# Attention and two expert layers on one core: later planning of the q, k, v loads, half as many filling products, new due times

## The chip, the cores and the metric

The kernel runs on one core of a Trainium2 chip, in one launch. The metric is the device time of that core in microseconds (us): the median of 3 runs before the change is 1045.23 us (1044.54 to 1047.05).

## What is computed

```python
scores = where(block_i >= block_j, q @ k.T / sqrt(64), -1e9)   # 4 batches, 8 heads, 576 positions, blocks of 64
attn   = exp(scores - max) / (sum + 1e-9)
x      = (attn @ v) as 2304 tokens x 512
h      = x @ moe_w_in                    # 512 -> 2048
x      = (h * tanh(softplus(h))) @ moe_w_out        # 2048 -> 512
h      = max(x @ moe2_w_in, 0)
out    = (h * h) @ moe2_w_out
```

## The kernel before, in words

The 2304 tokens are six chunks of 384. The first two chunks hold the low positions (0 to 191) of all four batches and are made by `attention_lo`, the other four the high positions, by `attention_hi`. Each chunk then goes through layer 1 and layer 2, in the twelve passes of `PASSES`; a pass is 16 steps, each of 12 products in `first_half` (line 1028, x by w_in) and 12 in `second_half` (line 1061, g by w_out), 128 x 384 each. Together these are 4608 products, called the main products below. Numbers are split in a high and a low half of 16 bits, so that each product is done three times.

**Weights.** The weights come as 64-bit floats. `unit` (lines 892 to 937) makes one of 32 units ready: a load of 1 MB into `raw` (line 895, two buffers), three passes of VectorE over 1024 columns (lines 905, 906, 908), a square on ScalarE (line 911), four norm products into the bank `spare` (line 915), their maximum on VectorE (line 922), a few tiny steps, and the two halves (lines 868 and 571).

**A head pair of the first two chunks** (`attention_lo`): loads of q and k (line 781, tile `qk`, two buffers) and of v (line 783, tile `vs`), the score products (line 791, tile `acc`), maxima on VectorE (lines 805 to 808), three exponentials on ScalarE into the single buffer `pl` (line 811), the scaling on GpSimd (line 577), the high half `pb` on ScalarE (line 553), the low half by a subtraction on GpSimd or VectorE (lines 559, 560), a transposing DMA (line 825), the products with v (line 760), and their copy to `xs` (line 770) with a maximum (line 772). There are 16 such pairs. Behind the eight pairs of a chunk stands `chunk_scale` (line 973).

**The order.** All instructions are tasks of a planner, class `Sched`. It has a duration for each task and a due place (`rank`) from tables at the end of the file (`W_AT`, `A_AT`, `ATT` and others). `forward` runs a list schedule over the engines with these durations, `backward` ranks the tasks by the latest start, and the program is written in the order of the planned starts. So each engine, and SyncE's queue of DMA issues, executes its tasks strictly in the planned order, whatever the real times are. For two kinds of operation the planner also chooses the engine.

**Filling products.** Where TensorE is planned to be idle, `fill` counts how many 128 x 128 products with the constant `ones` would go into the gap, and the writer emits that number ahead of the next task (line 1233). Their results go to the second half of the bank `spare` and are read by nobody.

```python
        t.fillers = n, where
...
    for t in seq:
        for _ in range(t.fillers[0] if t.fillers else 0):
            nc.tensor.matmul(out=spare[t.fillers[1]][:, 1, 0:128], lhsT=ones, rhs=ones, start=True, stop=True)
        t.fn()
```

Of the kernel before, what the change touches and what calls it, by code (L numbers as in the profile page):

```python
# [18 lines left out]
B, H, S, D = 4, 8, 576, 64  # L19
# [53 lines left out]

W_AT = [[[4000.0, 4500.0], [45000.0, 4500.0]]]

# [26 lines left out]


class Task:
    __slots__ = ("eng", "dur", "fn", "deps", "succ", "lat", "pos", "prio", "n", "ready", "start", "lock", "idx", "post", "after", "before", "opts", "fin", "why", "gen", "xpose", "first", "rank", "rows", "final", "fillers", "table", "mark")


class Sched:
# [7 lines left out]
    FIRST = {"PE": 300.0, "ACT": 1300.0, "DVE": 700.0}  # L116
    FILL, GUARD = 0.0, 300.0
    ROUNDS = 2


    SWITCH, HYST = 1300.0, 6000.0
# [19 lines left out]

    def add(self, eng, dur, fn, r=(), w=(), lat=0.0, lock=False, deps=(), pos=None, opts=(), table=None):
        t = Task()
        t.opts, t.table, t.mark = opts, table, None
        t.eng, t.dur, t.fn, t.lat, t.lock = eng, dur, fn, lat, lock
        t.deps, t.succ, t.pos, t.idx = set(deps), [], pos, len(self.tasks)
        t.after, t.before, t.rows, t.final, t.fillers = set(), [], 1.0, None, None
        for acc, write in ((r, False), (w, True)):
            for a in acc:
                inst, reg = a if isinstance(a, tuple) else (a, None)  # L150
                regs = list(set(inst.wr) | set(inst.rd)) if reg is None else [reg, None]
                for g in regs:
                    t.deps.update(inst.wr.get(g, ()))
                    if write:
                        t.deps.update(inst.rd.get(g, ()))
        for acc, write in ((r, False), (w, True)):
            for a in acc:
                inst, reg = a if isinstance(a, tuple) else (a, None)
                if not inst.tasks or inst.tasks[-1] is not t:
                    inst.tasks.append(t)  # L160
                if write:
                    if reg is None:
                        inst.wr, inst.rd = {None: [t]}, {}
                    else:
                        inst.wr[reg], inst.rd[reg] = [t], []
                else:
                    inst.rd.setdefault(reg, []).append(t)
        t.deps.discard(t)
        self.tasks.append(t)
        return t  # L170
# [13 lines left out]
    def fill(self, now, start, t, where):  # L184

        n = 0
        while True:
            f = Task()
            f.dur, f.rows = self.FILL, 1.0
            busy = dict(self.busy)  # L190
            self.clock(f, now)
            if now + f.dur > start - self.GUARD:
                self.busy = busy
                break
            now += f.dur
            n += 1
        t.fillers = n, where

    def build(self, order):
        for ring in self.rings:  # L200
# [79 lines left out]
    def forward(self):  # L280
# [32 lines left out]
        dma = xpose = 0.0  # L313
# [6 lines left out]
        while len(done) < len(self.tasks):  # L320
            best = None
            for name, (free, wait, ready) in engs.items():
                for q in (wait, ready):
                    while q and q[0][-1].start is not None:
                        heapq.heappop(q)
                if not wait and not ready:
                    continue
                now = max(free, blocked.get(name, 0.0)) if ready else max(free, wait[0][0])
                if best is None or now < best[0]:
                    best = (now, name)  # L330
            now, name = best
            e = engs[name]
            while e[1] and e[1][0][0] <= now:
                t = heapq.heappop(e[1])[2]
                if t.start is None:
                    heapq.heappush(e[2], (*key(t), t))
            t, skipped = None, []
            while e[2]:
                item = heapq.heappop(e[2])
                if item[-1].start is not None:  # L340
                    continue
                if item[-1].opts and better(item[-1], name, now):
                    skipped.append(item)
                    continue
                t = item[-1]
                break
            if name == "ACT" and t is not None and t.table and table and t.table != table:
                other = [i for i in e[2] if i[-1].start is None and i[-1].table in (None, table) and not i[-1].opts
                         and i[-1].rank < t.rank + self.HYST]
                if other:  # L350
                    heapq.heappush(e[2], (*key(t), t))
                    t = min(other)[-1]
            for item in skipped:
                heapq.heappush(e[2], item)
            if t is None:
                blocked[name] = now + 100.0
                e[0] = max(e[0], now)
                continue
            start = now

            if name == "DVE" and self.CONTEND:
                over = engs["POOL"][0] - now
                if over > 0:
                    t.dur += min(over, t.dur) * self.CONTEND[0] if t.lock else self.CONTEND[1] if t.dur < 130.0 else 0.0
            elif name == "POOL" and self.CONTEND:
                t.dur += max(0.0, min(engs["DVE"][0] - now, t.dur)) * self.CONTEND[2]
            if name == "ACT" and t.table and t.table != table:
                if table:
                    start += self.SWITCH
                    self.switches += 1  # L370
                table = t.table
            if not self.lock_model:
                pass
            elif name == "POOL":
                start = max(start, port[0])
            elif name == "DVE" and t.lock:
                start = max(start, port[1])
            if name == "PE":
                if t.final:
                    self.spare[t.final] = False  # L380
                place_ = [k for k, free in self.spare.items() if free]
                if place_ and self.FILL:
                    self.fill(e[0], start, t, place_[0])
            t.start = start
            if name == "PE":
                self.clock(t, start)
            end = start + t.dur
            if name == "POOL":
                port[1] = end
            elif name == "DVE" and t.lock:  # L390
                port[0] = end
            e[0] = end
            fin = end + t.lat
            if name == "SP":
                if t.xpose:
                    end = max(end, xpose + 170.0)
                dma = max(dma, end + 650.0 - (t.dur - t.gen)) + t.post
                if t.xpose:
                    xpose = dma
                e[0] = max(end, dma - self.AHEAD)  # L400
                fin = dma
            done.append(t)
            for k, s in enumerate(t.succ + t.before):
                s.n -= 1
                rt = fin + self.SEM[t.eng][s.eng] if k < len(t.succ) else start + 1.0
                if rt >= s.ready:
                    s.ready, s.why = rt, t
                if not s.n:
                    place(s)
# [28 lines left out]
def tile_attention_moe(ctx, tc, qk, qp, va, vd, w1, w2, out):  # L438
    nc = tc.nc
# [101 lines left out]
    def dma(fn, nbytes, r=(), w=(), issue=475.0, gen=475.0):  # L541
        t = sch.add("SP", issue, fn, r=r, w=w, lat=650.0 - (issue - gen) + nbytes / DMAR)
        t.post, t.gen, t.xpose = nbytes / DMAR, gen, issue > 1000
        return t
# [17 lines left out]
    def flat(t):  # L562
        return t.rearrange("p c k -> p (c k)")
# [211 lines left out]
    def attention_lo(b, h, x, xo, s_bank, av_bank):  # L775
# [2 lines left out]
        qs, vs, v3 = (R[k].new() for k in ("qk", "vs", "v3"))  # L778
        scale = 0.125
        cost = lambda m: c_mm(4 * m)  # L780
        dma(lambda: nc.sync.dma_start(qs.t[0:64, 0:4 * n].rearrange("p (a s) -> p a s", s=n), qk[b, h // 2].rearrange("d h a s -> d (h a) s")),
            1024 * n, w=[qs], issue=650.0, gen=650.0)
        dma(lambda: nc.sync.dma_start(flat(vs.t)[:, 0:6 * D], vd[b, :, h // 2].rearrange("p c k -> p (c k)")), 128 * 1536, w=[vs])
        thirds(vs, v3)

        pp, st = s_bank(0).new(), R["st"].new()
# [344 lines left out]
    n = NX  # L1131
# [115 lines left out]


L2_AT = [78800.0, 5000.0]
W_AT = [[[4300.0, 4300.0], [44000.0, 6800.0]]]  # L1250
C0_AT = 46000.0
C1_AT = 77500.0
A_AT = [[0.0, 16500.0], [44500.0, 73700.0], [75100.0, 150000.0]]
ATT = [[2, 2, 0, 0.0, 1.08], [3, 2, 1, 1.34, 2.57], [4, 5, 7, 0.47, 2.61], [5, 5, 8, 2.07, 4.28]]
Sched.SLACK = 0.98
Sched.HYST = 9200.0

# [56 lines left out]
```

## Time and profile before

| | |
|---|---|
| median of 3 runs | 1045.23 us (1044.54 to 1047.05) |
| the profiled execution | 1044.21 us, its span 1042.4 us |
| busy PE, DVE, ACT, POOL | 980.4, 648.0, 631.8, 175.6 us |
| mean granted TensorE clock | 0.98 |
| DMA | 153.83 MB, mean 148 GB/s |

All times of the trace are microseconds from the start of the span. A busy TensorE (PE) is not a useful one: the filling products count as busy, and a matmul's end is modelled, so that neighbouring products overlap in the rows. The granted clock is the share of full speed (1.0 is 2.4 GHz, 0.5 is 1.2 GHz) that the throttle gave TensorE; over a stretch it is a mean of these two levels. A releaser in brackets is what ended an engine's idle time.

### The profile page before, as it was taken

The page shows a single profiled execution, that of the slowest core. Times are in us where ns is not written, and L with a number is a line of the kernel's source. Part 1 is how long each engine was busy: PE and PEld are TensorE (multiplying, and loading weights), DVE is VectorE, ACT ScalarE, POOL GpSimd, SP SyncE. Part 2 cuts the span into 40 slices and gives each one's busy share as a digit, 9 for nine tenths or more (in the row PEclk, how much of TensorE's full clock was granted, in tenths as well). Part 3 has the DMA queues.
Part 4 walks back from the last instruction along what each step waited for, and adds up shares of the span by engine and source line. Part 5 has one row for each costly group of instructions (what it writes and reads, how often), then busy time and mean ns, then how long its engine had stood idle before and what let it go on. Part 6 is the DMA issues. An engine that isn't in the chain of part 4 may idle for free. (4 is left out here: it accounts for less than half of the span.)

```text
span 1042.4 us, 19262 instructions
## 1 busy us (share of the span) xinstructions
PE 980.4 (94%) x7409; PEld 612.7 (59%) x7409; DVE 648.0 (62%) x1539; ACT 631.8 (61%) x1157; POOL 175.6 (17%) x222
## 2 busy tenths in 40 slices
PE   8778888998999999999989999999899999999997
PEld 7677656666654555555545555655455566666664
DVE  5657987898989766786566378465675552141211
ACT  4435688665767666678765677565677753354443
POOL 2223732311212111211111011001121110000000
PEclk8889999999999999999999999999999999999999
DMA  7636796886646585585552256564755431122322
GB/s 231 149 82 188 203 280 195 268 297 222 256 135 157 133 189 132 138 196 151 133 127 67 82 143 144 119 160 140 173 130 130 86 97 62 61 81 82 112 80 92
DMA packets 150716, 153.83 MB, mean 148 GB/s; under 512 B 120160, under 2 KB 125280, under 8 KB 146528
## 3 DMA queue, kind: packets, MB, share of 16 engines
q1 hardware_dynamic: 150624, 152.60, 53.1%
q8 instruction: 58, 0.95, 0.4%
q14 instruction: 34, 0.28, 0.1%
HBM read 109.58 MB, written 14.16 MB: 119 GB/s over the span
## 5 line engine op out<-in xcount | busy, mean ns | idle before, releaser
L1061 PE MATMUL acc<-g,ws 128*128 128x384 f16 x2304 | 462.6, 326 | 3.8 <-DMA ws<-wspill 2.5
L1061 PEld LDWEIGHTS <-ws 128*128 128x128 f16 x2304 | 223.1, 98 | 152.8 <-issue 4.6
L571 DVE SCALAR_TENSOR_TENSOR g<-h,cst,g 128x384 f16<-128x384 f32 x192 | 120.7, 630 | 204.9 <-ACT g L868 159.5
L1028 PE MATMUL hp<-x,res 128*128 128x384 f16 x1152 | 234.2, 329 | 2.5 <-ACT h L1034 2.3
L1034 ACT ACTIVATE h<-hp,cst 128x384 f32<-128x384 f32 x192 | 110.0, 576 | 165.7 <-PE hp L1028 165.0
L1028 PE MATMUL hp<-x,late 128*128 128x384 f16 x864 | 181.6, 326 | 0.8 <-DVE cst L996 0.8
L1028 PEld LDWEIGHTS <-res 128*128 128x128 f16 x1152 | 110.7, 99 | 79.7 <-issue 12.4
L869 POOL TENSOR_SCALAR g<-h,cst 128x384 f16<-128x384 f32 x85 | 62.0, 731 | 378.7 <-PE acc L1061 160.8
L1028 PEld LDWEIGHTS <-late 128*128 128x128 f16 x864 | 81.5, 98 | 59.5 <-issue 7.9
L1233 PE MATMUL spare<-ones 128*128 128x128 bf16 x1205 | 88.5, 240 | 26.6 <-DVE wst L922 18.1
L1233 PEld LDWEIGHTS <-ones 128*128 128x128 bf16 x1205 | 82.9, 109 | 33.2 <-issue 22.2
L670 ACT ACTIVATE pf<-pab,st,sq 128x320 f32<-128x320 f32 (+2 forms) x96 | 67.3, 702 | 34.2 <-DVE st L665 29.6
L571 DVE SCALAR_TENSOR_TENSOR pb<-pf,st,pb 128x384 f16<-128x384 f32 (+2 forms) x96 | 72.4, 764 | 20.8 <-ACT pb L688 20.2
L868 ACT ACTIVATE g<-h,cst 128x384 f16<-128x384 f32 x107 | 65.6, 613 | 29.1 <-PE acc L1061 23.9
L688 ACT ACTIVATE pb<-pf,st 128x384 f16<-128x384 f32 (+2 forms) x96 | 64.9, 714 | 21.1 <-DVE st L681 7.6
L1028 PE MATMUL hp<-x,ws 128*128 128x384 f16 x288 | 59.6, 332 | 2.2 <-ACT h L1034 2.2
L662 DVE TENSOR_REDUCE st<-pab 128x2 f32<-128x640 f32 (+2 forms) x48 | 49.9, 1039 | 3.2 <-PE pab L654 2.3
L902 ACT ACTIVATE wf<-raw 128x1024 f32<-128x1024 f32 x32 | 36.5, 1141 | 21.6 <-DMA raw<-in_w_dram 10.6
L577 POOL TENSOR_SCALAR pl<-pl,st 128x192 f32<-128x192 f32 (+1 forms) x48 | 35.4, 751 | 75.0 <-DVE st L816 24.4
L981 POOL TENSOR_SCALAR x<-xs,cst 128x384 f16<-128x384 f32 x29 | 24.6, 862 | 122.6 <-DVE cst L863 112.2
L1039 ACT ACTIVATE h<-h 128x384 f32<-128x384 f32 x85 | 43.8, 515 | 1.1
L654 PE MATMUL pab<-q 64*128 64x320 f16 (+3 forms) x384 | 39.6, 307 | 3.7 <-DVE q L571 1.5
(120 smaller groups left out, 1072.0 us busy)
## 6 DMA issues: line engine op xcount, KB each, us to landing
ws<-wspill SPq DMA_DIRECT2D x108, 512.0 KB, 3.8
raw<-in_w_dram SPq DMA_DIRECT2D x32, 1024.0 KB, 6.0
wspill<-wn SPq DMA_DIRECT2D x18, 512.0 KB, 4.7
qk<-in_qp_dram SPq DMA_DIRECT2D x16, 480.0 KB, 4.1
vs<-in_va_dram SPq DMA_DIRECT2D x16, 320.0 KB, 3.9
out_dram<-ev SPq DMA_DIRECT2D x24, 192.0 KB, 2.1
qk<-in_qk_dram SPq DMA_DIRECT2D x16, 192.0 KB, 4.2
vs<-in_vd_dram SPq DMA_DIRECT2D x16, 192.0 KB, 3.7
```

Of the source, the lines that this page charges most:

```text
L571: return sch.add("DVE", c_dve(n) + 62 * ap, lambda: nc.vector.scalar_tensor_tensor(dst(), a(), s() if ap else s, c(), op0, op1), r=r, w=w, ...
L654: nc.tensor.matmul(out=pp.t[:, hd, o:o + k1 - k0], lhsT=qh.t[rows, u, a:a + 128], rhs=qh.t[rows, w, nq + k0:nq + k1], start=p == 0, stop=p ...
L662: sch.add("DVE", c_dve(2 * (o1 - o0)), lambda: nc.vector.reduce_max(both(st, j, r0), pp.t[r0:, :, o0:o1], axis=AX.X), w=[(pp, 0), (st, j)])
L670: sch.add("ACT", c_act(o1 - o0, True, 3), lambda hd=hd: nc.scalar.activation(pf[hd].t[r0:, k0:k0 + o1 - o0], pp.t[r0:, hd, o0:o1], AF.Exp, ...
L688: sch.add("ACT", c_act(n, False, 1), lambda pb=pb, pv=pv, s=s: nc.scalar.activation(pb.t[:, 0:i + 1, 0, :], pv(), AF.Copy, scale=s()), r=[ ...
L868: "ACT": ("ACT", c_act(n, False, 1), lambda: nc.scalar.activation(dst(0), src(), AF.Copy, scale=s()), False),
L869: "POOL": ("POOL", c_pool(n, False), lambda: nc.gpsimd.tensor_scalar(dst(0), src(), s(), 1.0, ALU.mult, ALU.mult), False),
L1028: nc.tensor.matmul(out=hp.t[:, 0:n], lhsT=w.t[:, f % 2, a, 128 * k:128 * k + 128], rhs=x.t[:, c, k, 0:n], start=k == 0 and i == 0, stop=k ...
L1034: sch.add("ACT", c_act(n, True, 1), lambda: nc.scalar.activation(h.t[:, 0:n], hp.t[:, 0:n], (AF.Mish, AF.Relu)[l], scale=hs()), r=[(cst, ( ...
L1039: "ACT": ("ACT", c_act(n), lambda: nc.scalar.activation(hv(), hv(), AF.Square), False),
L1061: nc.tensor.matmul(out=acc.t[:, 0:n], lhsT=wo.t[:, f % 2, a, 128 * m:128 * m + 128], rhs=g.t[:, c, 0:n], start=f == 0 and i == 0, stop=f = ...
L1233: nc.tensor.matmul(out=spare[t.fillers[1]][:, 1, 0:128], lhsT=ones, rhs=ones, start=True, stop=True)
```

## The change

Four edits in the planner and its tables; no operation of the kernel is added or taken away besides filling products.

- A task has a `slack`, in ns, that is added to the planned time at which it becomes ready behind each task that it waits for. The two loads of `attention_lo` get 4000 ns: they are planned 4 us after their buffer comes free, and those that find it free from the start are not moved by it.
- `fill` counts as before, and `SHARE` = 0.5 of the count, rounded down, is emitted.
- New numbers in `W_AT`, `C0_AT`, `A_AT`, `ATT` and `Sched.HYST`.

```diff
@@ class Sched
+    SHARE = 0.5
...
-        t.fillers = n, where
+        t.fillers = int(n * self.SHARE), where
...
-                rt = fin + self.SEM[t.eng][s.eng] if k < len(t.succ) else start + 1.0
+                rt = fin + self.SEM[t.eng][s.eng] + s.slack if k < len(t.succ) else start + 1.0
...
@@ def attention_lo
-        dma(lambda: nc.sync.dma_start(qs.t[0:64, 0:4 * n]...), 1024 * n, w=[qs], issue=650.0, gen=650.0)
-        dma(lambda: nc.sync.dma_start(flat(vs.t)[:, 0:6 * D], ...), 128 * 1536, w=[vs])
+        for t in (dma(...), dma(...)):
+            t.slack = 4000.0
...
-W_AT = [[[4300.0, 4300.0], [44000.0, 6800.0]]]
-C0_AT = 46000.0
+W_AT = [[[4300.0, 4600.0], [47800.0, 6800.0]]]
+C0_AT = 46400.0
-A_AT = [[0.0, 16500.0], [44500.0, 73700.0], [75100.0, 150000.0]]
-ATT = [[2, 2, 0, 0.0, 1.08], [3, 2, 1, 1.34, 2.57], [4, 5, 7, 0.47, 2.61], [5, 5, 8, 2.07, 4.28]]
+A_AT = [[0.0, 15000.0], [31700.0, 73700.0], [58000.0, 152100.0]]
+ATT = [[2, 2, 0, 0.0, 1.08], [3, 2, 1, 1.3, 2.54], [4, 5, 7, 0.47, 2.61], [5, 5, 8, 2.17, 4.35]]
-Sched.HYST = 9200.0
+Sched.HYST = 11200.0
```

The new program has 578 filling products where the old one has 1205. Of these 339 stand ahead of the scale product of the first chunk (line 973), where 707 stood. Ahead of the norm products of the 32nd and last weight unit stand 726 main products, where 702 stood. ScalarE's queue has 4 loads of its tables more. Line numbers of the changed file are higher by 1 to 3 in the rows below.

TensorE's queue around the first weight unit: the score products of the fourth head pair (tile `acc_1`) and the norm products of the unit (L915, L918 in the changed file). Before:

```order
L791 MATMUL acc_1_335<-qk_266 128x192
L791 MATMUL acc_1_335<-qk_266 128x64
L791 MATMUL acc_1_335<-qk_266 64x64
L791 MATMUL acc_1_335<-qk_266 128x192
L1233 LDWEIGHTS ones
L1233 MATMUL spare<-ones 128x128
L915 LDWEIGHTS onesq
L915 MATMUL spare<-wsq_333,onesq 128x256
```

After the change:

```order
L918 LDWEIGHTS onesq
L918 MATMUL spare<-wsq_269,onesq 128x256
L794 MATMUL acc_1_324<-qk_263 128x192
L794 MATMUL acc_1_324<-qk_263 128x64
L794 MATMUL acc_1_324<-qk_263 64x64
L794 MATMUL acc_1_324<-qk_263 128x192
```

The score products of that pair stood ahead of the unit's norm products and now stand behind them; the 69 filling products that followed the norm products before are now 23, and stand behind the score products.

SyncE's queue, its 4th to 13th entry: loads of q and k (`qk`), of v (`vs`), of weights (`raw`), and the first transposes of probabilities (`pt`). Before:

```order
L783 DMA vs_204<-in_vd_dram 128x384
L895 DMA raw_206<-in_w_dram 128x1024
L783 DMA vs_239<-in_vd_dram 128x384
L895 DMA raw_242<-in_w_dram 128x1024
L781 DMA qk_261<-in_qk_dram 64x768
L781 DMA qk_266<-in_qk_dram 64x768
L895 DMA raw_331<-in_w_dram 128x1024
L781 DMA qk_356<-in_qk_dram 64x768
L781 DMA qk_361<-in_qk_dram 64x768
L825 DMA_TRANSPOSE pt_368<-pb_350 128x7x128
```

After the change:

```order
L785 DMA vs_204<-in_vd_dram 128x384
L785 DMA vs_206<-in_vd_dram 128x384
L898 DMA raw_208<-in_w_dram 128x1024
L898 DMA raw_233<-in_w_dram 128x1024
L783 DMA qk_257<-in_qk_dram 64x768
L783 DMA qk_263<-in_qk_dram 64x768
L898 DMA raw_267<-in_w_dram 128x1024
L828 DMA_TRANSPOSE pt_333<-pb_318 128x7x128
L898 DMA raw_342<-in_w_dram 128x1024
L783 DMA qk_418<-in_qk_dram 64x768
```

The second load of v now stands ahead of both weight loads, and the q, k loads of the fifth and sixth pair (`qk_356`, `qk_361`, now `qk_418`, `qk_423`) stand behind the first transpose and the fourth weight load, ahead of which they stood.

The subtraction that ends the first pair's probabilities (`pb`). Before it stood on GpSimd, as the last of these rows:

```order
L559 TENSOR_TENSOR v_1_257<-v_1_257 128x384
L577 TENSOR_SCALAR pl_259<-pl_259,st_248 128x192 x2
L577 TENSOR_SCALAR pl_259<-pl_259,st_248 128x64
L559 TENSOR_TENSOR pb_350<-pl_259,pb_350 128x7x64
L577 TENSOR_SCALAR pl_365<-pl_365,st_255 128x192 x2
```

After the change it stands on VectorE:

```order
L909 SCALAR_TENSOR_TENSOR wf_259<-raw_233,wf_259 128x1024
L808 MEMSET acc_0_310 64x2x64
L561 TENSOR_TENSOR pb_318<-pl_245,pb_318 128x7x64
L809 TENSOR_REDUCE st_331<-acc_0_310 128x2
L911 SCALAR_TENSOR_TENSOR wf_259<-raw_233,wf_259 128x1024
L817 TENSOR_SCALAR st_247<-st_247 128x3
```

In the whole program 5 of the 16 such subtractions stay on GpSimd, where there were 9, and 11 stand on VectorE, where there were 7.

## Rows read from the trace of the kernel before

**Rows 1.** The page's first two parts: busy time, share of the span and instructions of PE and DVE; then, in 40 equal slices of the span, the granted TensorE clock in tenths.

```profile
PE 980.4 (94%) x7409; PEld 612.7 (59%) x7409; DVE 648.0 (62%) x1539; ACT 631.8 (61%) x1157; POOL 175.6 (17%) x222
...
PEclk8889999999999999999999999999999999999999
```

**Rows 2.** Busy time of each engine in three stretches of the span (us from its start): PE, weight loads, DVE, ACT, POOL, each with its instructions, then the granted clock, the share of the DMA engines and GB/s.

```profile
0.00:104.00 104.00, 83.87 (x1040) 75.20 (x1041) 64.45 (x159) 45.36 (x103) 30.39 (x41) 0.87 0.59 162
104.00:295.00 191.00, 173.19 (x1528) 117.58 (x1526) 171.05 (x364) 137.78 (x218) 60.27 (x63) 0.98 0.75 238
295.00:860.00 565.00, 546.14 (x3757) 313.45 (x3755) 370.87 (x934) 376.90 (x707) 83.78 (x116) 0.99 0.55 136
```

**Rows 3.** Line 1233, the filling products, alone, in the first two of these stretches: PE and PEld busy, granted clock, DMA share, GB/s of the whole stretch.

```profile
0.00:104.00 104.00, 55.70 (x719) 52.68 (x720) 0.87 0.59 162
104.00:295.00 191.00, 32.83 (x490) 30.20 (x487) 0.98 0.75 238
```

**Rows 4.** Waits of VectorE from 0 to 104 us: engine, tile and line that waited, what it waited for, us in total, times, the longest.

```profile
DVE acc L805 <- PE acc L791: 13.5, 6, 6.4
DVE wst L922 <- PE spare L915: 10.0, 2, 6.0
DVE v L560 <- DMA vs<-in_vd_dram: 6.1, 4, 3.7
DVE xm L772 <- ACT xs L770: 5.2, 1, 5.2
```

**Rows 5.** The timeline of VectorE between 26 and 94 us, the instructions that ended those waits: start, duration, engine, line, operation, tiles, shapes; in brackets the idle time before it and what ended it.

```profile
28.06 0.17 DVE L805 MEMSET acc<- 64x128 f32 x1 [6.36 <-PE acc L791]
...
44.90 0.17 DVE L805 MEMSET acc<- 64x128 f32 x1 [3.13 <-PE acc L791]
...
56.47 0.42 DVE L922 TENSOR_REDUCE wst<-spare 128x2 f32<-128x256 f32 x1 [5.97 <-PE spare L915]
...
59.11 0.17 DVE L805 MEMSET acc<- 64x128 f32 x1 [0.93 <-PE acc L791]
...
75.36 0.35 DVE L772 TENSOR_REDUCE xm<-xs 128x1 bf16<-128x192 f32 x1 [5.17 <-ACT xs L770]
...
89.39 0.42 DVE L922 TENSOR_REDUCE wst<-spare 128x2 f32<-128x256 f32 x1 [3.98 <-PE spare L915]
...
93.09 0.17 DVE L805 MEMSET acc<- 64x128 f32 x1 [1.21 <-PE acc L791]
```

**Rows 6.** The timeline of TensorE from 15 to 104 us, the runs of filling products (L1233) that stand ahead of those instructions, and two groups of norm products (L915).

```profile
17.20 1.06 PE L915 MATMUL spare<-wsq,onesq 128*128 128x256 bf16 x4
...
21.14 5.36 PE L1233 MATMUL spare<-ones 128*128 128x128 bf16 x69 [2.89 <-DVE wst L922]
...
27.90 0.61 PE L915 MATMUL spare<-wsq,onesq 128*128 128x256 bf16 x4
...
29.09 2.41 PE L1233 MATMUL spare<-ones 128*128 128x128 bf16 x40
...
36.53 5.09 PE L1233 MATMUL spare<-ones 128*128 128x128 bf16 x59 [2.68 <-DVE wst L922]
...
49.41 6.59 PE L1233 MATMUL spare<-ones 128*128 128x128 bf16 x70 [3.57 <-DVE wst L922]
...
68.21 6.09 PE L1233 MATMUL spare<-ones 128*128 128x128 bf16 x76 [5.24 <-DVE wst L922]
...
84.49 4.36 PE L1233 MATMUL spare<-ones 128*128 128x128 bf16 x47 [2.69 <-ACT pl L811]
```

**Rows 7.** The timeline of ScalarE, the square of the second weight unit, which the norm products at 27.90 us read.

```profile
20.78 1.06 ACT L911 ACTIVATE wsq<-wf 128x1024 bf16<-128x1024 f32 x1
```

**Rows 8.** The page's fifth part, by shape: the subtraction that makes the low half of the probabilities on VectorE and on GpSimd, and loads of ScalarE's tables. Behind the bar: busy us, mean ns of one.

```profile
L560 DVE TENSOR_TENSOR pb<-pl,pb 128x448 f16<-128x448 f32 x7 | 4.3, 620 | 2.5 <-ACT pb L553 2.4
...
L559 POOL TENSOR_TENSOR pb<-pl,pb 128x448 f16<-128x448 f32 x9 | 10.1, 1120 | 4.4 <-ACT pb L553 4.4
...
L1034 ACT ACT_TABLE_LOAD x26 | 33.4, 1283 | 2.8 <-DVE cst L1017 2.0 <-PE hp L1028 0.3
```

**Rows 9.** The chain that ended last, in order of time, one stretch near the end: start, us, what.

```profile
1027.46 8.79 PE acc L1061 x54
```

**Rows 10.** The timeline of TensorE: the norm products of the last weight unit.

```profile
294.29 0.60 PE L915 MATMUL spare<-wsq,onesq 128*128 128x256 bf16 x4
```

**Rows 11.** Busy time of each engine in two stretches of 5 us, columns as in group 2.

```profile
60.00:65.00 5.00, 2.54 (x46) 2.32 (x41) 3.43 (x12) 4.80 (x11) 0.90 (x2) 1.00 0.82 268
65.00:70.00 5.00, 1.79 (x18) 1.79 (x18) 5.00 (x10) 2.86 (x5) 2.44 (x3) 0.50 0.35 68
```

**Rows 12.** The timeline of SyncE: four of the first eight issues of the transpose that ends a head pair's chain through the one buffer pl.

```profile
19.63 1.34 SPq L825 DMA_TRANSPOSE pt<-pb  x1
...
76.48 1.23 SPq L825 DMA_TRANSPOSE pt<-pb  x1
...
83.80 1.23 SPq L825 DMA_TRANSPOSE pt<-pb  x1
...
95.88 1.22 SPq L825 DMA_TRANSPOSE pt<-pb  x1
```

**Rows 13.** Waits of the DMA queue of SyncE from 0 to 130 us, columns as in group 4.

```profile
SPq L781 <- PE acc L791: 41.1, 12, 11.0
```

**Rows 14.** The page's sixth part, the loads of q and k of the first two chunks: count, KB each, median us from issue to landing.

```profile
qk<-in_qk_dram SPq DMA_DIRECT2D x16, 192.0 KB, 4.2
```

More of the change, by code (lines that the diff above doesn't have):

```diff
@@ L104 @@
 class Task:
-    __slots__ = ("eng", "dur", "fn", "deps", "succ", "lat", "pos", "prio", "n", "ready", "start", "lock", "idx", "post", "after", "before", "opts", "fin", "why", "gen", "xpose", "first", "rank", "rows", "final", "fillers", "table", "mark")
+    __slots__ = ("eng", "dur", "fn", "deps", "succ", "lat", "pos", "prio", "n", "ready", "start", "lock", "idx", "post", "after", "before", "opts", "fin", "why", "gen", "xpose", "first", "rank", "rows", "final", "fillers", "table", "mark", "slack")
 class Sched:
@@ L143, in add @@
         t = Task()
-        t.opts, t.table, t.mark = opts, table, None
+        t.opts, t.table, t.mark, t.slack = opts, table, None, 0.0
         t.eng, t.dur, t.fn, t.lat, t.lock = eng, dur, fn, lat, lock
@@ L780, in attention_lo @@
         cost = lambda m: c_mm(4 * m)
-        dma(lambda: nc.sync.dma_start(qs.t[0:64, 0:4 * n].rearrange("p (a s) -> p a s", s=n), qk[b, h // 2].rearrange("d h a s -> d (h a) s")),
-            1024 * n, w=[qs], issue=650.0, gen=650.0)
-        dma(lambda: nc.sync.dma_start(flat(vs.t)[:, 0:6 * D], vd[b, :, h // 2].rearrange("p c k -> p (c k)")), 128 * 1536, w=[vs])
+        for t in (dma(lambda: nc.sync.dma_start(qs.t[0:64, 0:4 * n].rearrange("p (a s) -> p a s", s=n), qk[b, h // 2].rearrange("d h a s -> d (h a) s")),
+                      1024 * n, w=[qs], issue=650.0, gen=650.0),
+                  dma(lambda: nc.sync.dma_start(flat(vs.t)[:, 0:6 * D], vd[b, :, h // 2].rearrange("p c k -> p (c k)")), 128 * 1536, w=[vs])):
+            t.slack = 4000.0
         thirds(vs, v3)
```

## The prediction

> **What bounds the kernel now.** I read the page's first two parts, and they mislead: TensorE is busy 94% of the span at a clock near full speed [rows 1], as if nothing could be won ahead of its products. The windows correct this. From 0 to 104 us, before the first main product, TensorE is busy 83.87 us [rows 2], but 55.70 of these are filling products [rows 3]; its own work is 28.2 us. VectorE, which makes the weights ready and takes part in every step of attention, works 64.45 of these 104 us and stands still 39.5. From 104 to 295 us VectorE is the bound, with 171.05 of 191 us. The last weight unit comes at 294.3 us [rows 10]; from there TensorE is the bound, 546.14 of the next 565 us [rows 2], with no filling products. So the kernel is a front of 295 us paced by VectorE and a rest of 747 us paced by products. Time taken out of the front shifts the rest, and time lost in the front is not regained.
>
> Next, what VectorE waits for in the first 104 us [rows 4]: 13.5 us for score products, 10.0 for norm products, 5.2 for a copy that itself waits for products with v, 6.1 for loads of v. The timeline of VectorE gives the seven single waits that matter, 6.36, 3.13, 5.97, 0.93, 5.17, 3.98 and 1.21 us, 26.8 in all [rows 5]. The timeline of TensorE shows what it did meanwhile: filling products, every time [rows 6]. The clearest is the second weight unit. Its square ends at 21.84 us [rows 7], its norm products start at 27.90, and from 21.14 to 26.50 TensorE runs 69 filling products [rows 6]. A queue is executed in order, so a run planned for a gap pushes real work back when the gap is not there. Two things make it so: all five runs of 47 and more in these rows began only when TensorE was let go by VectorE or ScalarE, 2.68 to 5.24 us after it went idle (the run's own bank had to be read first), and one product takes 60 ns in the fastest of the rows (2.41 us for 40), 86 and 94 in two of those runs (5.09 for 59, 6.59 for 70) [rows 6].
>
> **The change, step by step.** The sum is made against the profiled execution, 1044.2 us (its span 1042.4 and 1.8 around it), which lies 1.0 below the median of the runs, 1045.2.
>
> *Half the filling products.* Ahead of the first chunk's scale product 339 remain of 707. I take each run at half its time, and let each wait shrink by that half or to nothing: 6.36 less 2.7 (run of 5.36), 3.13 less 3.1 (5.09 and a shorter one), 5.97 less 3.3 (6.59), 5.17 less 3.0 (6.09), 3.98 less 2.2 (4.36), and I take 0.7, a third, for 0.93 and 1.21 together [rows 5, 6]. That is **15.0 us**. Bounds: nothing, if each wait finds another releaser, and 26.8, if all seven go. The upper bound is checked by the next limit, the single buffer `pl`, through which the head pairs pass one after the other: the transposes that close a pair were issued 7.32 us apart at best, and seven steps took 76.25 us [rows 12]; seven of the best would take 51.2, so not over 25.0 us can be won. After 104 us the runs are shorter, 32.83 us in 191 [rows 3], VectorE is busy beside them, and I count nothing there.
>
> *Subtractions on VectorE.* Five more of VectorE's two-operand operations on 128-partition tiles stand ahead of the last unit (four of them the subtractions of `pb`), at about 0.62 us each where GpSimd took 1.12 [rows 8]: **+3.1 us** on the engine that bounds the front. Bounds: 0, where they fall into its idle time, and 3.1.
>
> *Main products earlier.* At the last weight unit 24 more main products stand behind TensorE. One costs 0.163 us at full pace (54 in 8.79 us [rows 9]), so the rest is shorter by **3.9 us**; the front has room, 17.8 us of idle TensorE and half of 32.83 us of filling products [rows 2, 3]. Bounds: 0 and 3.9.
>
> *Loads later in the queue.* SyncE stood 41.1 us before loads of q and k whose buffer TensorE had not released [rows 13], with whatever followed in its queue. The new order puts transposes and weight loads ahead of such loads. What VectorE could gain is what it lost to loads, 6.1 us, less the 3.7 of the first load, for which nothing can be done [rows 4]: between 0 and 2.4, I take **1.2**. That the later loads make score products late is a rival below.
>
> *The clock.* TensorE fell to half speed five times in the front already: from 60 to 65 us it was busy 2.54 of 5 us at full clock, and the next 5 us were granted 0.50 [rows 11]. Fewer filling products leave more such stretches. Own work ahead of 104 us is 28.2 us at a mean of 0.87 [rows 2, 3]; at a mean of 0.75 it would be 32.7, and half of that difference on the path is **+2 us**. The duration at either level is in the rows: a group of norm products took 1.06 us at 17.20 and 0.61 at 27.90 [rows 6]. Bounds: 0 and +20.9, all of it at half and on the path (28.2 x 0.87 / 0.5 less 28.2).
> The Trainium skill speaks against the change here: TensorE: Matmul & The Clock Gate, section "Part 1: The HAM clock gate (the 'warmup' mystery)", says that the throttled clock is the default and that only activity releases it. By that rule alone the sum would take the term's upper end and come out near the time before; the rows agree with the rule in kind, but show the clock at 0.98 from 104 to 295 us, where filling products are 17% of the time.
>
> *Tables and the later passes.* Four more loads of 1.28 us on ScalarE [rows 8], which is busy 376.90 of 565 us in the part bounded by TensorE [rows 2]: nothing, hidden behind main products; 5.1 us if each fell between a product and its reader. The new due times of the later chunks move attention by a few steps between main products that stay as many: nothing, 3 us either way.
>
> Sum: -15.0 + 3.1 - 3.9 - 1.2 + 2 = -15.0, so 1029.2 for the profiled execution and **1030 us** for the median.
>
> **The rivals.**
> - *All the waits go.* With the runs short enough, work is never pushed back, and ScalarE, which was blocked behind the same products, runs ahead too. For it: every one of the seven waits ends behind a run. Against: runs of up to 47 are left. 25.0 instead of 15.0, all of the loads' 2.4 and no loss to the clock: 1030 - 10.0 - 1.2 - 2, **1017 us**.
> - *The wait moves to the loads.* The q, k loads of the fifth and later pairs now stand behind a transpose, which waits for the pair's whole chain. If three score products then wait for a load of 4.2 us, the median to landing [rows 14], 12.6 us come back: **1043 us**, no change that can be told. For it: SyncE's queue is strictly in order [rows 13]. Against: a load needs 4.2 us and a pair at least 7.32 [rows 12, 14], so one load can hide.
> - *The clock stays at half, in the front and beyond.* This is the case that ends slower. If the front loses 10 us to it (half the bound), and the stretch from 104 to 295 us runs two fifths of its own product work at half clock, then 140.4 us of work at 0.98 grow by 0.4 x 137.6 = 55 us, of which idle time and removed filling products cover 17.8 + 16.4 = 34 [rows 2, 3]. 1030 - 2 + 10 + 21: **1059 us**. It decides the sign once the two together pass 17 us; the middle stretch adds nothing until a quarter of its work runs at half (34 of 137.6). For it: rows 11. Against: in that stretch TensorE would still be busy 82% of the time (140.4 and 16.4 of 191), and 0.98 was granted at 91%.
>
> **How the numbers follow.** A measurement of this kernel cannot tell less than 0.3%, 3.1 us, from no change. The forecast gets 0.58, and by its own bounds it lies between 1020 and 1037. All waits gone: 0.14. Waits moved to the loads: 0.13, half of it over 0.3% faster, half within it. The clock: 0.15, of which 0.01 ends within 0.3%. So faster 0.58 + 0.14 + 0.06 = 0.78, same 0.07 + 0.01 = 0.08, slower 0.14. The range runs from 1012 (all waits gone, with 26.8 for 25.0 and the later passes' 3 us on top) to 1046 (the moved wait, with those 3 us against it); it leaves out the clock's case and a little below.
>
> **What would show it.** Right: the first scale product some 15 us earlier, near 88 us, VectorE idle some 25 us before it instead of 39.5, none of its waits behind score or norm products over 4 us, the last weight unit near 281 us instead of 294.3, and the rest as long as before, 743 to 748 us. The clock's mean up to the scale product should be between 0.7 and 0.85. Wrong in its first step: the same waits of 4 to 6 us with TensorE idle, not filling. Wrong for the loads: score products that wait for `qk` several us each. Wrong for the clock: a mean under 0.65 in the front and under 0.85 from there to the last unit.

## The result and the profile after

The changed kernel took 1013.68 us (median of 5 runs, 1011.07 to 1019.69), the kernel before 1044.54 in the same comparison (5 runs, 1044.06 to 1047.05): a ratio of 0.9704, 95% interval 0.9672 to 0.9736, or 30.9 us. The forecast was 15 us, in the right direction and half the size. The profiled execution of the change is the slowest of the five (1019.69, span 1017.9; its mean granted clock is 0.967, that of the other four 0.976 to 0.979), so its rows account for 24.5 of the 30.9 us.

Where those 24.5 lie: the first scale product came at 84.3 us instead of 103.3, the norm products of the last weight unit at 277.8 instead of 294.3 [rows 10], and the rest took 740.1 us instead of 748.1. So 16.5 us come from the front and 8.0 from the rest.

The page's first parts, as [rows 1]:

```profile
PE 955.5 (94%) x6782; PEld 582.4 (57%) x6782; DVE 643.4 (63%) x1544; ACT 640.8 (63%) x1168; POOL 161.8 (16%) x210
...
PEclk8877899999999999999999999999999999999999
```

The three stretches, cut at the scale product and the last unit; columns as in [rows 2]:

```profile
0.00:84.30 84.30, 62.84 (x651) 52.00 (x652) 60.44 (x158) 44.27 (x102) 29.66 (x41) 0.82 0.68 190
84.30:277.80 193.50, 173.35 (x1307) 112.09 (x1305) 170.92 (x370) 138.95 (x222) 51.70 (x57) 0.93 0.75 239
277.80:860.00 582.20, 566.65 (x3890) 326.61 (x3888) 377.26 (x951) 393.62 (x729) 78.92 (x110) 0.99 0.54 134
```

The filling products (now L1236) in the first two, as [rows 3], then the last unit, as [rows 10]:

```profile
0.00:84.30 84.30, 29.36 (x339) 27.04 (x339) 0.82 0.68 190
84.30:277.80 193.50, 20.05 (x242) 17.80 (x239) 0.93 0.75 239
...
277.81 0.60 PE L918 MATMUL spare<-wsq,onesq 128*128 128x256 bf16 x4
```

Ahead of the scale product VectorE works 60.44 us and idles 23.9; before, it worked 64.2 and idled 39.1 of 103.3. What it waits for there, as [rows 4]: score products fell from 13.5 us to 2.7, norm products from 10.0 to 7.3, with no single wait for either over 3.1. The 5.2 us for the copy to `xs` are 0.3 now. A wait for ScalarE's first step on the weights (`wf`) has grown from 0.7 to 4.6.

```profile
DVE wst L925 <- PE spare L918: 7.3, 3, 3.1
DVE v L561 <- DMA vs<-in_vd_dram: 5.3, 3, 3.8
DVE wf L908 <- ACT wf L905: 4.6, 3, 3.0
DVE acc L808 <- PE acc L794: 2.7, 5, 1.2
```

One thing in [rows 6] I had noted but not priced: the runs of filling products were held. Their results go to one half of the tile `spare`; VectorE reads the norms of a weight unit from the other half (`wst`, line 922). The program makes TensorE wait for that reader before the first filling product. This is what TensorE waited for from 0 to 104 us, in the kernel before and then in the change:

```profile
PE spare L1233 <- DVE wst L922: 14.9, 5, 5.2
```

```profile
PE spare L1236 <- DVE wst L925: 6.2, 4, 2.5
...
PE acc L794 <- DMA qk<-in_qk_dram: 9.0, 6, 3.2
```

TensorE's waits for loads of q and k went the other way, to 9.0 us from 0.5. So the change has shorter holds as well as shorter runs, and the experiments ask which of the two was worth what.

### The profile page after: what moved, and what is told of

Same layout as the page of the kernel before. It is cut to its first block, busy times and chain, and to the rows that moved or that the text cites. A ratio compares the mean times of both kernels' runs of the same rounds, so it can differ in the third digit from the quotient of the medians.

```text
span 1017.9 us, 18009 instructions
## 1 busy us (share of the span) xinstructions
PE 955.5 (94%) x6782; PEld 582.4 (57%) x6782; DVE 643.4 (63%) x1544; ACT 640.8 (63%) x1168; POOL 161.8 (16%) x210
## 5 line engine op out<-in xcount | busy, mean ns | idle before, releaser
L1031 PE MATMUL hp<-x,late 128*128 128x384 f16 x864 | 183.8, 330 | 1.7 <-DVE cst L999 1.7
L872 POOL TENSOR_SCALAR g<-h,cst 128x384 f16<-128x384 f32 x82 | 64.9, 792 | 391.2 <-PE acc L1064 165.9
L689 ACT ACTIVATE pb<-pf,st 128x384 f16<-128x384 f32 (+2 forms) x96 | 65.0, 713 | 20.5 <-issue 8.3
L1236 PE MATMUL spare<-ones 128*128 128x128 bf16 x578 | 49.4, 255 | 12.3 <-DVE wst L925 8.7
L1236 PEld LDWEIGHTS <-ones 128*128 128x128 bf16 x578 | 44.8, 117 | 19.0 <-issue 13.9
L794 PE MATMUL acc<-qk 64*128 64x192 f32 (+2 forms) x128 | 33.6, 389 | 12.2 <-DMA qk<-in_qk_dram 9.0
L761 PEld LDWEIGHTS <-v 128*64 128x64 f16 (+1 forms) x736 | 36.4, 115 | 10.9 <-issue 5.2
## 6 DMA issues: line engine op xcount, KB each, us to landing
out_dram<-ev SPq DMA_DIRECT2D x24, 192.0 KB, 2.3
qk<-in_qk_dram SPq DMA_DIRECT2D x16, 192.0 KB, 4.9
vs<-in_vd_dram SPq DMA_DIRECT2D x16, 192.0 KB, 4.3
```

Source lines behind the costliest of these rows:

```text
L689: sch.add("ACT", c_act(n, False, 1), lambda pb=pb, pv=pv, s=s: nc.scalar.activation(pb.t[:, 0:i + 1, 0, :], pv(), AF.Copy, scale=s()), r=[ ...
L761: nc.tensor.matmul(out=out, lhsT=v, rhs=p, start=edge[0], stop=edge[1])
L872: "POOL": ("POOL", c_pool(n, False), lambda: nc.gpsimd.tensor_scalar(dst(0), src(), s(), 1.0, ALU.mult, ALU.mult), False),
L1031: nc.tensor.matmul(out=hp.t[:, 0:n], lhsT=w.t[:, f % 2, a, 128 * k:128 * k + 128], rhs=x.t[:, c, k, 0:n], start=k == 0 and i == 0, stop=k ...
```

## The experiments

Ratios are to the kernel before, run on the same chip in the same comparison (medians 1044.54 us for the change, 1042.61 for e1 to e4, 1045.46 for e5 to e8, 1041.74 for e9 to e12, 1041.02 for e13 and e14); "c1" is the start of the first scale product, "last unit" that of its norm products, both from the profile.

| | us | ratio, 95% | c1 | last unit |
|---|---|---|---|---|
| before | 1044.54 | 1 | 103.3 | 294.3 |
| the change | 1013.68 | 0.9704 (0.9672 to 0.9736) | 84.3 | 277.8 |
| e1 before, half the fillers | 1030.68 | 0.9883 (0.9838 to 0.9928) | 93.8 | 284.1 |
| e2 change, all fillers | 1019.53 | 0.9782 (0.9741 to 0.9822) | 87.1 | 280.4 |
| e3 before + allowance for loads | 1031.69 | 0.9892 (0.9854 to 0.9931) | 85.1 | 276.6 |
| e4 before + new tables | 1028.89 | 0.9868 (0.9824 to 0.9912) | 92.3 | 279.3 |
| e5 loads later in the queue only | 1094.28 | 1.0461 (1.043 to 1.0491) | 135.8 | 341.9 |
| e6 plan of e3, loads not later | 1036.27 | 0.9903 (0.9875 to 0.9932) | 85.2 | 280.2 |
| e7 before, no fillers | 1022.63 | 0.9776 (0.9753 to 0.9799) | 82.8 | 272.9 |
| e8 change, no fillers | 1016.78 | 0.9717 (0.9699 to 0.9736) | 81.4 | 274.2 |
| e9 before, fillers in a free bank | 1017.45 | 0.9768 (0.9722 to 0.9814) | 78.8 | 267.9 |
| e10 change, all, free bank | 1010.19 | 0.9699 (0.9658 to 0.9741) | 80.1 | 272.1 |
| e11 change, half, free bank | 1009.69 | 0.9689 (0.9636 to 0.9742) | 77.8 | 270.0 |
| e12 before + front's tables | 1036.51 | 0.994 (0.9918 to 0.9962) | 89.7 | 281.7 |
| e13 before, one filler a gap | 1028.28 | 0.9895 (0.9833 to 0.9958) | 87.7 | 275.4 |
| e14 change, fillers in front only | 1014.56 | 0.9746 (0.9696 to 0.9795) | 81.4 | 272.7 |

### The parts, one at a time

**e1** is the kernel before with the halving alone:

```diff
-        t.fillers = n, where
+        t.fillers = int(n * 0.5), where
```

> The kernel before, its order kept to the instruction, with half of each run of filling products. Theory F (runs of filling products push real work back in the queue): most of the gain is here, 18 to 27 us, so 1018 to 1026 us. Theory P (the new plan, loads later in the queue and new due times, makes the gain): at most 5 us, 1039 to 1045 us.

**e2** is the changed kernel with `SHARE = 1.0`.

> The changed kernel, its order kept, with all filling products that its planner counts. Theory F: most of the gain is lost again, 1032 to 1040 us. Theory P: it stays, 1014 to 1020 us.

**e3** is before with the 4000 ns `slack` on the two loads and nothing else, **e4** before with the new numbers of the tables and nothing else.

> The kernel before with the loads of q, k, v of the first two chunks planned 4 us after their buffer comes free, old tables, all filling products. Theory F: 1038 to 1048 us. Theory P with the loads as the cause: 1015 to 1030 us.

> The kernel before with the new due times and the new HYST, loads planned as before, all filling products. Theory F: 1038 to 1048 us. Theory P with the due times as the cause: 1015 to 1030 us.

The halving alone is worth 1.2% (12 us), less than my 15 and between the ranges of the two theories. The new order with all filling products is worth 2.2% (23 us), where my sum had about 2 us; that is theory P. On the new order the halving adds only 0.8%. The allowance and the tables each gain over 1% by themselves, e4 in theory P's range and e3 1.7 us beyond it. So the term that I had called nearly nothing was the larger one; but what it was worth *through*, these four don't tell. In e2 VectorE's waits for norm products are still 12.6 us up to 85 us, and 7.3 in the change; that is where the halving acted.

TensorE's waits for the reader of `wst`, 0 to 104 us, in e1 and in e2:

```profile
PE spare L1233 <- DVE wst L922: 15.8, 6, 5.6
```

```profile
PE spare L1236 <- DVE wst L925: 7.6, 4, 3.1
```

They were 14.9 us before and are 6.2 in the change. The halving leaves the holds as they are, and the new order takes half of them away.

### Is it the queue of loads or the plan of the products?

The allowance moves loads in SyncE's queue, and lets the planner move everything that hangs on them. **e5** keeps the order of the other four engines and every filling product, and moves the loads in the queue by up to 4 us of the plan (the lines with a minus are those of e3):

```diff
+        key = {t: t.start + t.move for t in self.tasks}
...
+            if t.eng != "SP":
+                if t.eng in chains:
+                    nxt[chains[t.eng]] = t
...
-            t.slack = 4000.0
+            t.slack, t.move = 0.0, 4000.0
```

The program is written in the order of `key`, and every engine but SyncE keeps its planned order.

**e6** is the reverse: the plan made with the allowance, and the loads moved back by 4000.

> The kernel before with one thing changed: the loads of q, k, v of the first two chunks stand up to 4 us of the plan later in SyncE's queue (16 loads change places with their neighbours there). The order of TensorE, VectorE, ScalarE and GpSimd, and every filling product, is that of before. Before was 1042.6 us in the last comparison; the whole 4 us allowance, which also lets the planner move the products and the vector work, gave 1031.7. Theory Q (the allowance works because SyncE no longer stands 41 us behind loads whose buffer isn't free): nearly all of the gain is here, 1031 to 1035 us, and SyncE's waits on q, k loads for the score products fall under 15 us. Theory P (it works because the products are planned where their data really are, and the queue was never what anyone waited for): 1040 to 1044 us, though SyncE's waits fall all the same.

> The complement: the order of TensorE, VectorE, ScalarE and GpSimd that the planner makes with the 4 us allowance, all filling products of that plan, old tables, but the loads of q, k, v stand 4 us of the plan earlier in SyncE's queue again, where their buffer would be free by the plan. The full allowance gave 1031.7 us, before 1042.6. Theory Q (queue): 1038 to 1043 us, SyncE's waits for the score products back above 25 us. Theory P (plan of the products): 1030 to 1034 us.

Theory P held, and the queue alone did worse than either theory said: 49 us slower. Waits of TensorE in e5 from 0 to 136 us, and of SyncE's queue (L918 is the load of raw weights there, L848 the transpose):

```profile
PE spare L1256 <- DVE wst L945: 24.1, 5, 9.7
PE acc L814 <- DMA qk<-in_qk_dram: 14.7, 4, 8.0
```

```profile
SPq L918 <- DVE wf L931: 42.5, 4, 13.8
SPq L848 <- DVE pb L581: 29.2, 3, 16.8
```

SyncE's waits did not go away; it now stands behind transposes and weight loads, with the loads that the next score products need queued behind them. My rival of the moved wait is real if the products stay where they were: score products wait 14.7 us for their loads, near the 12.6 that I had put, but the whole costs 49 us. e6 has nearly all the gain of e3 (0.9903 against 0.9892; its 1036.27 us are 2.3 over theory P's range, with a kernel before that took 2.9 longer than beside e3) without the later places, and SyncE waits 16.0 us for score products again, against 6.2 in e3 (theory Q had over 25). So "loads later" wins nothing as a queue order alone, and the gain is in the order of the other engines. What shows in it is that the holds on `wst` fall to 8.4 us in e3 and in e6, from 14.9; that the gain goes through them is argued, since neither plan was run without filling products. The line of e3:

```profile
PE spare L1236 <- DVE wst L925: 8.4, 5, 2.1
```

### What a filling product costs

**e7** and **e8** leave all filling products out of either order (`t.fillers = 0, where`).

> Before's order with no filling product at all (half of them gave 1030.7 us against 1042.6 for all). Theory L (a filling product costs its own time, and the clock that it holds up is worth little): another 8 to 12 us less than half of them, 1019 to 1023 us, first scale product near 86 us. Theory C (half of the fillers already gives back part of what it saves, in half-speed stretches of 37 and 21 us up to the last weight product): the second half saves no more than it costs, 1028 to 1040 us, with over 60 us at half speed ahead of the first scale product.

> The changed kernel's order with no filling product (all: 1019.5 us, half: 1013.7). Theory L: 1006 to 1010 us. Theory C: 1013 to 1025 us, with over 60 us at half speed ahead of the first scale product and more than the changed kernel's 27 us between it and the last weight product.

In before's order the second half is worth nearly as much as the first (1.1% after 1.2%): theory L, 1022.63. In the changed order leaving out the other half changes nothing that can be told (0.9717 against 0.9704), and 1016.78 us lies in theory C's range: e8 doesn't tell apart what the products still cost there and what the clock costs without them. So the change took out most of what filling products cost, and the two orders without any differ by 0.6% only (0.9776 and 0.9717). That is what the new order is worth for itself; the other 1.6% of its 2.2 were losses to fillers that it avoided.

The table says where these 0.6% lie. Without filling products the last unit stands at 272.9 us in before's order and at 274.2 in the changed one, so for itself the new order wins nothing in the front; the rest takes 747.4 us in e7 and 740.3 in e8.

**e9** keeps before's order and all 1205 filling products, and gives those ahead of the first task that uses the banks `hp` one of these:

```diff
-                nc.tensor.matmul(out=spare[t.fillers[1]][:, 1, 0:128], lhsT=ones, rhs=ones, start=True, stop=True)
+                nc.tensor.matmul(out=hps[1][:, 0:128] if free else spare[t.fillers[1]][:, 1, 0:128], lhsT=ones, rhs=ones, start=True, stop=True)
...
+            free = free and t not in used
```

> Before's order and all of its filling products, with one thing changed: ahead of the first main product the filling products are written to a bank that nobody reads or writes yet (hp1) instead of to the tile whose other half VectorE still reads. In the profile of before the filling products of the first 104 us waited 14.9 us for that reader (line 922, wst), 2.7 and 0.9 for ScalarE, and ran their whole count afterwards. Theory D (a run does harm because it begins late, held by its own tile's reader, and then stands ahead of work that is ready): the first scale product comes 12 to 18 us earlier than 103.3, the kernel takes 1026 to 1034 us. Theory N (a run costs what it takes wherever it begins, so only its number counts): within 4 us of before, 1039 to 1047.

Theory D, and beyond its range: 0.9768, as much as leaving them out, at the same number. TensorE's timeline in e9 where [rows 6] have the second unit of before:

```profile
17.76 4.01 PE L1235 MATMUL hp<-ones 128*128 128x128 bf16 x69
21.75 1.50 PE L791 MATMUL acc<-qk 64*128 64x192 f32 x8
23.19 0.61 PE L915 MATMUL spare<-wsq,onesq 128*128 128x256 bf16 x4
```

The same 69 products start at 17.76 us instead of 21.14, straight behind the work ahead of them. At full clock (the norm group just ahead of them takes 0.60 us, 1.06 in [rows 6]) they take 4.01 us instead of 5.36, and the norm products stand at 23.19 instead of 27.90. Over the front the hold is gone (0 to 104 us):

```profile
PE spare L1235 <- DVE wst L922: 1.4, 3, 0.6
```

Was the hold itself the loss, or the run behind it? **e13** keeps the tile and the hold and emits one product a gap:

```diff
-        t.fillers = n, where
+        t.fillers = min(n, 1), where
```

> Before's order and its shared tile, but a single filling product in each gap (48 in all for 1205). Each still waits for the reader of its tile, so TensorE's queue is held as before; what goes is the run that follows. Theory R (the run that stands behind the hold does the harm, since what is queued behind it has become ready by then): as without any filling product, 1019 to 1025 us. Theory H (the hold itself does the harm: score and norm products that are ready stand behind a TensorE that waits 15 us for VectorE): 1028 to 1036 us, with the waits for line 922 still over 12 us.

TensorE's waits for the reader, 0 to 104 us in e13:

```profile
PE spare L1233 <- DVE wst L922: 15.0, 6, 5.8
```

The hold is back in full, and c1 stands at 87.7, between the 82.8 of no filler and the 103.3 of all. By that, of 20.5 us in the front the hold costs 4.9 and the runs behind it 15.6. This is an estimate: e13's front runs at half speed like e7's (a group of norm products takes 1.01 to 1.06 us), that of before mostly at full speed. The whole time, 1028.28, and the 15.0 us of waits are in theory H's range, but 3.8 us of the time lie behind the last unit, where neither kernel has a filling product: the same 4852 products take 725.09 us there in e13 and 721.93 in e7, at a granted clock of 0.99 and 1.00. Both parts count, the run more.

### On the changed order

**e10** and **e11** give the fillers of the changed kernel's front the free bank, with all of them and with half; **e14** has all of them there and none behind the first main product.

> The changed order with all filling products (1019.5 us with the shared tile), those ahead of the first main product in the bank that nobody reads. Theory D: the fillers of the front cost nearly nothing, first scale product at 81 to 84 us instead of 87.1, 1012 to 1017 us. Theory N: 1018 to 1021.

> The changed kernel (half of the filling products), with those ahead of the first main product in the bank that nobody reads. Theory D: first scale product at 80 to 83 us instead of 84.3, 1009 to 1013 us, faster than both kernels. Theory N: 1013 to 1017, as the changed kernel.

> The changed order with all filling products of the front in the bank that nobody reads, and none behind the first main product (1010.2 us with those too, which go to the shared tile). If the runs in the shared tile cost the middle stretch as they cost the front: 1002 to 1008 us, the stretch from the first scale product to the last weight unit under 189 us (192.0 with them). If VectorE paces that stretch either way: 1009 to 1014 us and 190 to 194 us.

With the free bank it no longer matters whether half or all are emitted, and 1010 us is the best that was run. In both c1 came earlier than theory D's range had it; e11's time is in that range, e10's 1.8 us below. By the ratios the two are ahead of the change by 0.5 and 1.6 us, and their intervals overlap its own, so a gain over it is not shown. In e14 the middle stretch (c1 to the last unit) takes 191.3 us against 192.0 in e10: VectorE paces it either way, as expected, though the time of 1014.56 us lies 0.6 us over the range for that case.

**e12** is before with the due times of the front alone (`W_AT`, `C0_AT`, `A_AT`).

> Before with the new due times of the front alone (W_AT, C0_AT, A_AT); ATT and HYST old, no allowance for the loads, all filling products. All new tables together gave 1028.9 us. If their gain lies in the steps of the front: 1027 to 1033 us, first scale product near 92 us. If it lies in the later chunks' places and ScalarE's tables: 1037 us and more.

It is faster, by less than all tables: c1 comes 13.6 us earlier, but the rest grows to 753.4 us from 748.1, against 747.8 in e4. VectorE's waits for norm products up to c1 are 1.7 us in e12 and 1.6 in e4, 10.0 before; its waits for score products stay (12.4 and 13.1 us against 13.5). So the front's due times shorten the front, and what goes there is the waits for norm products. That `ATT` and `HYST` keep this from being lost later rests on one profile of each, and how they would do it is open.

## Why the prediction was half right

**The step that failed** is the price of the new order: by my sum its terms came to 2 us (+3.1, -3.9 and -1.2, and nothing more for the due times), and measured with all filling products it was worth 23 us (e2). I had the terms stand side by side, as if an order could not change what a filling product costs. It did: with filling products left out the two orders are 0.6% apart, so most of the 23 us are losses to filling products that the new order avoids.

**What bounds the kernel: right.** Time won in the front moved the rest, the middle stretch stayed VectorE's (170.92 us of work in 193.5, against [rows 2]), and TensorE bounds the rest. The marks that I had set were met: c1 at 84.3 for 88, VectorE idle 23.9 for 25, no score or norm wait over 4 us, last unit at 277.8 for 281, clock 0.82 up to c1 (with the doubt of the last section). One was not: the rest is 740.1 us, not 743 to 748. That c1 met its mark is in part luck: I had the halving alone bring it there, which brings it to 93.8 (e1); the rest of the way is the order's.

**Half the filling products, -15.0: the mechanism right, the price made of the wrong thing.** I gave each wait back half of its run. Measured in the same order it was 12 us, and the whole (none, or all in a free bank) 23 to 24 us, close under the 25.0 and 26.8 of my bounds. What failed is that I let this term stand apart from the new order, and took the halved count as all that could shrink. I had written that five runs began 2.68 to 5.24 us late because their tile was being read, and priced only their length. A late run is what does harm: the same number of them, not held, cost nothing that can be told (e9 against e7). The re-plan shortens the holds, the halving shortens the runs, and together they remove most of the loss. The time comes nearest to my rival "all the waits go", 1017 us, which I gave 0.14; but 10.0 of the 23.5 us that VectorE waited for score and norm products stay, so its condition is met in part only, and by the order as much as by the shorter runs that it names.

**Loads later, -1.2 (0 to 2.4): wrong, and the bounds too.** I priced the places in the queue. These alone cost 49 us (e5); the allowance as the planner uses it gains 11 (e3), nearly all of it by the order of the other engines (e6). In the change itself TensorE waits 9.0 us for these loads, 0.5 before, six times and 3.2 us at most: my sign of being wrong for the loads showed in part, and VectorE's waits for score products fell all the same. I looked for the effect of a number in the planner on the engine that it names, and not on all the tasks behind it.

**Subtractions on VectorE, +3.1: the size right, the effect not seen.** The eleven subtractions of `pb` take 7.7 us in the change, the seven of before 4.3 [rows 8]. The middle stretch grew by 2.5 us, but VectorE is no busier up to the last unit: 60.44 and 170.92 us in the two stretches, against 64.23 and 170.58 before. Its three passes over the weights (lines 905, 906 and 908) took 101.4 us there in place of 105.4, at 32 each; why, no run shows.

**Main products earlier, -3.9: right, and something came on top.** TensorE's busy time behind the last unit fell by 4.7 us, with 24 main products fewer (before, then the change):

```profile
294.30:1042.40 748.10, 724.05 (x4852) 420.52 (x4850) 413.17 (x1019) 449.36 (x839) 84.92 (x118) 0.99 0.47 122
```

```profile
277.80:1017.90 740.10, 719.33 (x4829) 418.27 (x4826) 412.06 (x1018) 457.62 (x847) 80.44 (x112) 0.99 0.48 124
```

The other 3.3 us are idle time: 24.1 us before, 20.8 now. It is a balance of many waits; the largest that shrank is that for one step of a later pass, by 3.0 us in the same stretches of before and of the change. I had put the later passes at nothing, 3 us either way. The gain in the rest is no accident of one execution: the six runs of the changed order take 736.1 to 740.3 us behind the last unit, and before's order with any number of filling products 745.0 to 751.2.

```profile
PE hp L992 <- ACT nsq L987: 4.7, 2, 4.0
```

```profile
PE hp L995 <- ACT nsq L990: 1.7, 2, 1.2
```

**The clock, +2 (0 to 20.9): small as forecast, the path wrong.** What the clock costs in the change itself no run separates. Without fillers the products of the front run at half speed throughout (below): TensorE's busy time there is 47.87 us, against 27.4 for the same work in e9 (72.66 less 45.24 of fillers). These 20.5 us are near my upper bound of 20.9. But c1 is only 4.0 us later, 82.8 against 78.8: TensorE is not what the front waits for once nothing stands in its way. (e9 differs by its filling products too; their own cost and the clock's are taken together here.) So the rival of the cold clock, 1059 us, was far off: the coldest runs took 1022.63 (e7) and 1016.78 (e8). The Trainium skill says in TensorE: Matmul & The Clock Gate, section "Part 1: The HAM clock gate (the 'warmup' mystery)", that the throttled state is the default and activity releases it. e7 agrees on the state: its groups of norm products take 1.01 to 1.04 us up to c1, 0.60 or 0.61 in e9. It shows that this cost little time here.

**Tables, 0: wrong for the due times.** I priced ScalarE's loads of tables and the later chunks, and for the front's due times only the subtractions and main products that they move. The new numbers alone gain 13.7 us with all filling products (e4). For the loads of tables: in the same stretches TensorE waits 6.7 us for ScalarE's exponentials (`pf`) in the change, 2.3 in the kernel before. Whether the further loads of tables cause that was not tried; the idle time as a whole fell all the same.

## What to carry to other kernels

Work that is only there to keep an engine warm must not wait for anything: give its result a place that no other engine touches, and look in the trace for idle time *ahead* of it. Here its harm lay in when it ended more than in how long it was, so first ask why it begins late, and only then how much of it to cut. When an edit changes a planner's number, price every queue that the new plan moves; the engine that the number names may be the one where it does nothing.

## What was not expected of the hardware

The profile's column of the granted clock reads 1.00 where the trace has no record of a level yet. e7, its window to c1, and one group of four norm products in it:

```profile
0.00:82.80 82.80, 47.87 (x320) 35.38 (x321) 63.71 (x158) 44.05 (x101) 27.91 (x41) 1.00 0.69 194
...
19.27 1.04 PE L915 MATMUL spare<-wsq,onesq 128*128 128x256 bf16 x4
```

The same in e9, where the clock was granted in full:

```profile
0.00:78.80 78.80, 72.66 (x1027) 64.47 (x1028) 63.72 (x158) 44.17 (x101) 29.84 (x41) 1.00 0.76 208
...
17.33 0.60 PE L915 MATMUL spare<-wsq,onesq 128*128 128x256 bf16 x4
```

Both windows read 1.00, and a group takes 1.04 us in one and 0.60 in the other. A clock of 1.00 at the start of a program should be checked against the duration of a known product; the same holds for the 0.87 that I took for the first 104 us of before, and for the change's 0.82: both read 1.00 up to 15 us, and the first group of norm products behind that takes 1.06 us in before (at 17.20) and 1.04 in the change (at 18.29).

The wait of the fillers seems to be the program's, not the memory's. Ahead of the result I called `spare` a bank; the code makes it a tile of two halves of 512 values, and they write a half of `spare` that the reader doesn't touch. The Trainium skill, PSUM — Partial Sum Buffer, section "Terms", gives a bank 2 KiB in each partition, so that a half of 512 fp32 values is as large as a bank. No run here split that tile, so that this half alone would have been enough is not shown.
